# Attention scores and products with v take turns on all eight PSUM banks; weight loads are paced; one engine rounds q and k

## The chip, the core and the metric

The kernel runs on one core of a Trainium2 chip. Its time is the device time of the program in microseconds, the median of several runs; one execution is also taken by the hardware profiler. A core has TensorE (PE; its weight loads are listed as PEld), VectorE (DVE), ScalarE (ACT), GpSimd (POOL, idle here) and SyncE (SP, whose queue issues every DMA here). TensorE writes to PSUM, which has eight banks of 2 KB for each of 128 partitions; one matmul output of 512 fp32 columns fills a bank.

## What is computed

Sigmoid attention over 8 batches, 12 heads, 448 positions and 64 columns, followed by a gated MLP over the 3584 rows:

```python
scores = np.matmul(q, k.transpose(0, 1, 3, 2)) / np.sqrt(64) - np.log(448)
attn = 1.0 / (1.0 + np.exp(-scores))
x = np.matmul(attn, v).transpose(0, 2, 1, 3).reshape(3584, 768)
h = x @ w_in                                # 768 x 2048
g = h * (1.0 / (1.0 + np.exp(-1.702 * h)))
out = g @ w_out                             # 2048 x 768
```

The weights reach the kernel as 64-bit words; it decodes them to fp32 on the chip.

## The kernel before, in words

**The planner.** Nothing is issued while the code walks the loops. Each step becomes a task with an engine (or two to choose from, `either`), an estimated cost, the tasks that it needs and the buffers that it uses. Buffers of one tag form a ring: with BUFS[tag] slots, a buffer's users wait for all users of the one that many places earlier (lines 104 to 106). `Plan.run` (line 92) then plays the tasks through a model of the engines and emits each engine's instructions in the order in which the model begins them, which is the fixed order of that engine's queue on the chip. TensorE takes units in order from two streams, the attention ("side") and the MLP ("main"). Another engine takes, among the tasks that are ready, the one with the smallest key: its place in TensorE's order, or that of the first task that waits for it (`keys`, line 228). VectorE prefers tasks that only it can do (line 190), unless a task with a smaller key than that, and due within SOON places of TensorE's current one, is ready or nearly so (lines 193 to 199). The model lets a DMA land 2.2 us after its transfer, counted at 0.0027 us for each KB, and 1.5 us later still for the 64-bit weights (lines 46 and 387).

**The attention** handles 48 pairs of heads (8 batches by 6 pairs). A pair's q and k arrive as one tile (`qkraw`, line 479) and are split into a rounded part (line 340 on ScalarE or 341 on VectorE, by the planner's choice) and the rest (line 346, VectorE), so that three matmuls of fp32r make one precise product; only the very first pair is multiplied unsplit. The scores of a pair are made in four chunks of 112 keys: each is 6 matmuls, two heads side by side on 64 rows each, into a double bank (line 518). One sigmoid for each chunk (line 529) goes from the double bank to SBUF tile `a` (3 buffers of two chunks). The product with v (line 541, 16 matmuls on all four chunks, two heads side by side on 64 columns each) follows one pair later: a unit of TensorE's order is the four chunks of scores of pair n, then the product of pair n - 1. One or two copies (line 575 on ScalarE or 577 on VectorE) take it from PSUM to the blocks of x, which are 512 rows and so don't coincide with batches; finished blocks are spilled to DRAM.

PSUM holds two double banks `sc` and one `sc3`, which the chunks take in turn (every third one `sc3`), and the single banks `av` and `m0`, which the products with v take in turn. That makes all eight. After the attention `sc3` is closed and gives two single banks `m`; the MLP's first block takes `m0`, `m`, `m` in turn.

**The weights** come in 32 pieces, 16 for the down matrix first, then 16 (index below NF) for the up matrix. `decode` (line 372) loads a piece of 768 KB into one of three `raw64` buffers, makes it fp32 in seven VectorE steps (one of them free to go to ScalarE) and one of ScalarE (line 397), and stores it to DRAM (`stored`, line 430). The load waits for its buffer alone; its key is that of a pair's rounding, pair 2 + int(1.3 x piece). In the attention, sums and differences of down pieces are also made, split and stored (line 642), for a Strassen-like scheme in the later blocks.

**The MLP** is one block of 512 rows by plain products (`mlp`, lines 686), then three rounds of two blocks by seven products in place of eight (`two_blocks`, lines 918 and 1059).

Of the kernel before, what the change touches and what calls it, by code (L numbers as in the profile page):

```python
# [9 lines left out]
F32 = mybir.dt.float32  # L10
# [6 lines left out]
U64 = mybir.dt.uint64  # L17
# [7 lines left out]

PACE = 1.3

# [6 lines left out]
BUFS = dict(  # L34
    qk=2, vraw=3, a=3, x32=8, x=6, g=16, line=4, wsplit=3, raw64=3, w32=2, e=3,
    sc=2, sc3=1, av=1, m=2, m0=1,
    xs=15, xa=4,
)

ATTENTION, LATE = ("qk", "vraw", "a", "raw64", "e"), ("xs", "xa")  # L40
SHARED = ("line",)


# [199 lines left out]
def sigmoid_attention_mlp(ctx: ExitStack, tc: tile.TileContext, qk, v, w, out):  # L243
# [30 lines left out]

    for tag in ("sc", "av", "m0"):
        banks(tag, ctx)
    banks("sc3", early_bank)
    ctx.callback(early_bank.close)
# [20 lines left out]
    nc.vector.memset(still, 1.0)  # L299
    ps = spaces["m0"].tile([P, 512], F32, tag="m0", name="still", bufs=BUFS["m0"])  # L300
    for n in range(WARM):
# [4 lines left out]
    def make(b, tag, shape, dtype, name):  # L306
        if tag == "m" and tag not in spaces:
            early_bank.close()
            banks(tag, early_bank)
        if tag in LATE and tag not in spaces:  # L310
            att_stack.close()
            late = late_stack.enter_context(tc.tile_pool(name="late", bufs=2))
            for t in LATE:
                spaces[t] = late
        b.tile = spaces.get(tag, sb).tile(shape, dtype, tag=tag, name=name, bufs=BUFS[tag])
        return b.tile
# [20 lines left out]
    def round_and_rest(costs, b, src, deps, uses, hi, lo, first=lambda: None):  # L337

        c = on_either(
            (costs[0], lambda: nc.scalar.copy(hi(), src())),  # L340
            (costs[1], lambda: nc.vector.tensor_copy(hi(), src())),
            deps, [b, *uses], first,
        )
        return task(
            "DVE", costs[2],
            lambda: nc.vector.tensor_tensor(lo(), src(), hi().bitcast(F32), op=ALU.subtract),  # L346
            [c], [b, *uses],
        )
# [23 lines left out]
    def decode(n):  # L372
# [12 lines left out]

        load = dma(lambda: raw.tile.bitcast(U64), lambda: w[n], 2 * KB, [], [raw], take)
        load.landing += 1.5
        plan.early.append((load, firsts[min(2 + int(PACE * len(decoded)), len(firsts) - 1)]))

# [39 lines left out]
        decoded[n] = (t_p, f, f32)  # L429
        stored[n] = dma(lambda: whole[n], f32, KB, [t_p], [f])  # L430

# [53 lines left out]
    def split_pair(b, p, t_q, qkr):  # L485
        if (b, p) == (0, 0):
            return t_q, qkr
        s = buffer("qk")
        t = round_and_rest(
            (0.94, 0.63, 1.09), s, lambda: qkr.tile, [t_q], [qkr],  # L490
            lambda: s.tile[:, 0], lambda: s.tile[:, 1],
            lambda: make(s, "qk", [P, 2, S2], F32R, f"qk{b}_{p}"),
        )
        return t, s


    chunks = itertools.count()
    last_early = []

    def scores(b, p, c, t_s, s, a):  # L500

        tag = "sc"
        if next(chunks) % 3 == 2:
            tag = "sc3"
        ps = buffer(tag)
        if tag == "sc3":
            last_early[:] = [ps]

# [4 lines left out]
        def emit():  # L513
            make(ps, tag, [P, 2, 512], F32, f"sc{b}_{p}_{c}")
            src = [s.tile] if plain else [s.tile[:, 0], s.tile[:, 1]]
            for n, (kk, qq) in enumerate(terms):
                for j, rows in enumerate(halves_of_rows):
                    nc.tensor.matmul(  # L518
                        ps.tile[:C, j, :S],
                        lhsT=src[kk][rows, S + c * C : S + (c + 1) * C], rhs=src[qq][rows, :S],  # L520
                        start=n == 0, stop=n == len(terms) - 1,
                    )

        t = task("PE", 0.9 if plain else (0.7, 0.61, 0.61, 0.7)[c], emit, [t_s], [ps, s])

# [8 lines left out]

    def values(b, p, c, t_a, a, t_v, vr, ps, bank):

        def emit():
            if c == 0:
                make(ps, bank, [P, 512], F32, f"av{b}_{p}")
            for j, cols in enumerate(halves_of_rows):  # L540
                nc.tensor.matmul(  # L541
                    ps.tile[cols, :S], lhsT=vr.tile[:C, j, c], rhs=a.tile[:C, c % 2, j],
                    start=c == 0, stop=c == NC - 1,
                )

        return task("PE", (0.8, 0.75, 0.75, 0.85)[c], emit, [t_a, t_v], [ps, a, vr])
# [24 lines left out]
    def to_x(b, p, t, ps):  # L571
        for block, xb, first, into, cols in x32_places(b, p):
            n = cols.stop - cols.start
            wrote[block, p].append(on_either(
                (0.2 + 0.00075 * n, lambda xb=xb, into=into, cols=cols: nc.scalar.copy(
                    xb.tile[:, into], ps.tile[:, cols])),
                (0.15 + 0.00105 * n, lambda xb=xb, into=into, cols=cols: nc.vector.tensor_copy(
                    xb.tile[:, into], ps.tile[:, cols])),
                [t], [xb, ps], first,
            ))  # L580
        split_x(b, p)
# [20 lines left out]
    def attention():  # L602

        units, late = [], []
        for n, (b, p) in enumerate(pairs):
            t_q, qkr, t_v, vr = load_pair(b, p)
            t_s, s = split_pair(b, p, t_q, qkr)
            bank = "av" if n % 2 else "m0"
            ps = buffer(bank)
            scored, next_late = [], []  # L610
            firsts.append(t_s)
            for half in range(2):
# [3 lines left out]
                next_late.append([  # L616
                    values(b, p, 2 * half + i, g[1], a, t_v, vr, ps, bank) for i, g in enumerate(got)
                ])

            for t in scored[1]:  # L620
                t.alone = False
            units.append(scored[0] + scored[1] + [t for two in late for t in two])
            to_x(b, p, next_late[1][1], ps)
            late = next_late
        units.append(late[0] + late[1])
        return units
# [47 lines left out]
    def product_bank():  # L674

        n = next(groups)
        return ("m", last_early[0].users if n < 3 else []) if n % 3 else ("m0", [])

    def mlp(b):
# [11 lines left out]
        for f in range(NF):  # L691
            t_w, wb = wsplit(f)
            bank, edge = product_bank()
            ps = buffer(bank)
            g, gb = buffer("line"), buffer("g")
            for part in range(3):
                ks = range(2 * part, 2 * part + 2)

                def emit(ks=ks, part=part, ps=ps, bank=bank, wb=wb, f=f):
                    if part == 0:  # L700
                        make(ps, bank, [P, 512], F32, f"h{b}_{f}")
                    for k in ks:
                        product(ps.tile, wb.tile, k, xs[b, k][1].tile, k == 0, k == NK - 1)

# [5 lines left out]

            def sigmoid(g=g, ps=ps, f=f):
                make(g, "line", [P, T], F32, f"g{b}_{f}")
                nc.scalar.activation(g.tile, ps.tile, AF.Sigmoid, scale=1.702)

            t = task("ACT", 0.6, sigmoid, [t], [g, ps])
            t = task(
                "DVE", 0.69,
                lambda g=g, ps=ps: nc.vector.tensor_tensor(g.tile, ps.tile, g.tile, op=ALU.mult),
                [t], [g, ps],
# [452 lines left out]
```

## Time and profile before

| | us |
|---|---|
| median of 3 runs | 1117.43 (1116.3 to 1117.65) |
| the profiled execution | 1117.21 |
| its span, first to last instruction | 1115.4 |
| TensorE busy | 1107.6 |
| VectorE busy | 759.4 |
| ScalarE busy | 508.1 |
| attention, until the MLP's first matmul | 295.5 |

A row of busy time gives its share of the span. The attention, the first block of the MLP and the three rounds of two blocks follow one another on TensorE. Matmuls are pipelined: a matmul's record is longer than the time until the next one starts, so a busy TensorE is not proof that it steps at full pace, and starts have to be compared.

### The profile page before, as it was taken

The page shows a single profiled execution, that of the slowest core. Times are in us where ns is not written, and L with a number is a line of the kernel's source. Part 1 is how long each engine was busy: PE and PEld are TensorE (multiplying, and loading weights), DVE is VectorE, ACT ScalarE, POOL GpSimd, SP SyncE. Part 2 cuts the span into 40 slices and gives each one's busy share as a digit, 9 for nine tenths or more (in the row PEclk, how much of TensorE's full clock was granted, in tenths as well). Part 3 has the DMA queues.
Part 4 walks back from the last instruction along what each step waited for, and adds up shares of the span by engine and source line. Part 5 has one row for each costly group of instructions (what it writes and reads, how often), then busy time and mean ns, then how long its engine had stood idle before and what let it go on. Part 6 is the DMA issues. An engine that isn't in the chain of part 4 may idle for free.

```text
span 1115.4 us, 14973 instructions
## 1 busy us (share of the span) xinstructions
PE 1107.6 (99%) x5517; PEld 819.6 (73%) x5517; DVE 759.4 (68%) x1234; ACT 508.1 (46%) x729; POOL 0.2 (0%) x4
## 2 busy tenths in 40 slices
PE   8999999999999999999999999999999999999998
PEld 3544544545688888888888888888888888888887
DVE  6999999895496426887984664448864744477652
ACT  6988988888563322223633222225432322244220
POOL 0000000000000000000000000000000000000000
PEclk9999999999999999999999999999999999999999
DMA  9999999995455968666777975567669755556665
GB/s 330 333 375 375 388 400 395 385 338 162 151 188 182 358 216 321 246 244 216 254 227 223 307 242 191 195 198 250 216 208 310 255 188 191 195 174 214 207 202 194
DMA packets 113097, 285.69 MB, mean 256 GB/s; under 512 B 10368, under 2 KB 51328, under 8 KB 113024
## 3 DMA queue, kind: packets, MB, share of 16 engines
q1 hardware_dynamic: 113024, 284.73, 74.6%
q8 instruction: 44, 0.72, 0.3%
q14 instruction: 29, 0.24, 0.1%
HBM read 206.05 MB, written 78.64 MB: 255 GB/s over the span
## 4 chain that ended last, share of the span: by engine, by line
PE 96%; ACT 1%; DMA 1%; issue 0%; DVE 0%; SPq 0%; ACTq 0%; DVEq 0%
PE os L1059 18%; PE m L918 18%; PE oa L1059 13%; PE av L541 13%; PE sc L518 11%; PE sc L918 9%; PE h L686 6%; PE o L686 6%; PE av L918 4%; DMA qkraw<-qk 1%; ACT a L529 1%; SPq L321 0%; ACT sign L397 0%; DVE qk L346 0%; ACT qk L340 0%
## 5 line engine op out<-in xcount | busy, mean ns | idle before, releaser
L529 ACT ACTIVATE a<-sc,bias 112x896 f32<-112x896 f32 x192 | 183.0, 1006 | 42.8 <-PE av L541 30.4
L1059 PE MATMUL os<-gs,wds 128*128 128x512 f32 x864 | 196.3, 389 | 0.0
L1059 PEld LDWEIGHTS os<-gs,wds 128*128 128x128 f32 x864 | 162.2, 188 | 33.7
L541 PE MATMUL av<-a,vraw 112*64 112x448 f32 x768 | 154.7, 545 | 0.0
L1059 PE MATMUL oa<-ga,wda 128*128 128x512 f32 x648 | 147.4, 389 | 0.0
L1059 PEld LDWEIGHTS oa<-ga,wda 128*128 128x128 f32 x648 | 121.6, 188 | 25.3
L518 PE MATMUL sc<-qk 64*112 64x448 f32 x1128 | 137.4, 378 | 2.2 <-ACT a L529 2.1
L518 PEld LDWEIGHTS sc<-qk 64*112 64x112 f32 x1128 | 90.9, 171 | 63.3 <-ACT a L529 52.0
L541 PEld LDWEIGHTS av<-a,vraw 112*64 112x64 f32 x768 | 50.9, 136 | 82.3 <-issue 73.4
L918 PE MATMUL m<-x_s,w 128*128 128x512 f32 x468 | 109.3, 389 | 0.0
L918 PE MATMUL sc<-x,w 128*128 128x512 f32 x432 | 105.7, 389 | 0.0
L918 PEld LDWEIGHTS m<-x_s,w 128*128 128x128 f32 x468 | 87.8, 188 | 18.2
L918 PEld LDWEIGHTS sc<-x,w 128*128 128x128 f32 x432 | 81.1, 188 | 16.8
L880 ACT ACTIVATE g<-h 128x512 f32<-128x512 f32 x72 | 44.7, 632 | 91.1 <-DVE h L781 90.3
L340 ACT CAST gs<-gs 128x512 fp32r<-128x512 f32 x75 | 46.6, 623 | 84.5 <-PE os L1059 74.5
L686 PE MATMUL h<-x,wsplit 128*128 128x512 f32 x288 | 65.6, 389 | 0.0
L686 PE MATMUL o<-gs,wsplit 128*128 128x512 f32 x288 | 65.4, 389 | 0.0
L686 PEld LDWEIGHTS h<-x,wsplit 128*128 128x128 f32 x288 | 54.0, 188 | 11.9 <-issue 0.7
L686 PEld LDWEIGHTS o<-gs,wsplit 128*128 128x128 f32 x288 | 54.1, 188 | 11.2
L346 DVE TENSOR_TENSOR gs<-gs,gs 128x512 fp32r<-128x512 f32 x96 | 60.9, 686 | 0.4
L885 DVE TENSOR_TENSOR gs<-sc,g 128x512 f32<-128x512 f32 x24 | 16.6, 692 | 60.6 <-ACT g L880 60.6
L346 DVE TENSOR_TENSOR qk<-qkraw,qk 128x896 fp32r<-128x896 f32 x47 | 51.2, 1089 | 6.2 <-ACT qk L340 5.5
(94 smaller groups left out, 1204.1 us busy)
## 6 DMA issues: line engine op xcount, KB each, us to landing
w<-w SPq DMA_DIRECT2D x56, 768.0 KB, 6.6
wds<-t SPq DMA_DIRECT2D x72, 384.0 KB, 4.1
t<-t SPq DMA_DIRECT2D x32, 768.0 KB, 5.4
w<-t SPq DMA_DIRECT2D x32, 768.0 KB, 5.0
qkraw<-qk SPq DMA_DIRECT2D x48, 448.0 KB, 9.3
wda<-w SPq DMA_DIRECT2D x48, 384.0 KB, 4.0
f<-w SPq DMA_DIRECT2D x32, 384.0 KB, 8.1
w<-wsplit SPq DMA_DIRECT2D x16, 768.0 KB, 6.1
```

Source lines behind the costliest of these rows:

```text
L340: (costs[0], lambda: nc.scalar.copy(hi(), src())),
L346: lambda: nc.vector.tensor_tensor(lo(), src(), hi().bitcast(F32), op=ALU.subtract),
L518: nc.tensor.matmul(ps.tile[:C, j, :S], lhsT=src[kk][rows, S + c * C : S + (c + 1) * C], rhs=src[qq][rows, :S], start=n == 0, stop=n == len ...
L529: nc.scalar.activation(a.tile[:C, c % 2], ps.tile[:C, :, :S], AF.Sigmoid, bias=bias[:C], scale=scale)
L541: nc.tensor.matmul(ps.tile[cols, :S], lhsT=vr.tile[:C, j, c], rhs=a.tile[:C, c % 2, j], start=c == 0, stop=c == NC - 1,)
L686: nc.tensor.matmul(ps, lhsT=ws[a], rhs=x[:, c], start=first and i == 0, stop=last and i == 2)
L880: nc.scalar.activation(g.tile, h(), AF.Sigmoid, scale=1.702)
L885: nc.vector.tensor_tensor(gb.tile[:, block - one], h(), g.tile, op=ALU.mult)
L918: nc.tensor.matmul(ps, lhsT=ws[c], rhs=x[:, d], start=not more and i == 0 and j == 0, stop=i == NK // 2 - 1 and j == 2, skip_group_check=more,
L1059: nc.tensor.matmul(to, lhsT=w[c], rhs=x.tile[:, d], start=not more and i == 0 and j == 0, stop=i == len(rows) - 1 and j == 2, skip_group_c ...
```

## The change

- The chunks of scores and the products with v share one rotation over four double banks, in the order in which the units are formed: `sc`, `sc`, `sc3`, `sc4`. A product takes the turn after the four chunks of the next pair. `av`, `m0` and `m` are opened when the first MLP product needs one; by then `sc3` and `sc4` are closed. The MLP's first product takes a bank of `sc`, and the three after it wait for the last users of `sc3` and `sc4`.
- q and k are rounded by VectorE alone (cost None for ScalarE).
- A weight load is due with pair 2 + int(1.45 x piece) and waits for the rounding of pair int(1.45 x piece) - 1.
- The store of a piece of the up matrix waits for the rounding of the sixth last pair.
- The exponent buffers `e` are four in place of three; some of the planner's costs change; the planner looks only at a unit's first two chunks of scores to decide when it can begin.

```diff
-PACE = 1.3
+PACE, LEAD = 1.45, 1
+LATEST = 6
...
-    qk=2, vraw=3, a=3, x32=8, x=6, g=16, line=4, wsplit=3, raw64=3, w32=2, e=3,
-    sc=2, sc3=1, av=1, m=2, m0=1,
+    qk=2, vraw=3, a=3, x32=8, x=6, g=16, line=4, wsplit=3, raw64=3, w32=2, e=4,
+    sc=2, sc3=1, sc4=1, av=1, m=2, m0=1,
...
+EARLY, SINGLE = ("sc3", "sc4"), ("m0", "av", "m")
...
-    for tag in ("sc", "av", "m0"):
-        banks(tag, ctx)
-    banks("sc3", early_bank)
+    banks("sc", ctx)
+    for tag in EARLY:
+        banks(tag, early_bank)
...
-        if tag == "m" and tag not in spaces:
+        if tag in SINGLE and tag not in spaces:
             early_bank.close()
-            banks(tag, early_bank)
+            for t in SINGLE:
+                banks(t, early_bank)
...
-        load = dma(lambda: raw.tile.bitcast(U64), lambda: w[n], 2 * KB, [], [raw], take)
+        pair = int(PACE * len(decoded))
+        load = dma(lambda: raw.tile.bitcast(U64), lambda: w[n], 2 * KB, [firsts[pair - LEAD]] if pair >= LEAD else [],
+                   [raw], take)
         load.landing += 1.5
-        plan.early.append((load, firsts[min(2 + int(PACE * len(decoded)), len(firsts) - 1)]))
+        plan.early.append((load, firsts[min(2 + pair, len(firsts) - 1)]))
...
-        stored[n] = dma(lambda: whole[n], f32, KB, [t_p], [f])
+        stored[n] = dma(lambda: whole[n], f32, KB, [t_p, *(firsts[-LATEST:][:1] if n < NF else [])], [f])
...
-            (0.94, 0.63, 1.09), s, lambda: qkr.tile, [t_q], [qkr],
+            (None, 0.63, 1.09), s, lambda: qkr.tile, [t_q], [qkr],
...
+    def two_banks(b):
+        b.tag = ("sc", "sc", *EARLY)[next(turns) % 4]
+        plan.rings.setdefault(b.tag, []).append(b)
+        last_early[b.tag] = b
...
     def scores(b, p, c, t_s, s, a):
-        tag = "sc"
-        if next(chunks) % 3 == 2:
-            tag = "sc3"
-        ps = buffer(tag)
+        ps = Buffer()
+        two_banks(ps)
...
-            for t in scored[1]:
+            if n:
+                two_banks(before)
+            before = ps
+
+            for t in scored[1] + [t for two in late for t in two]:
                 t.alone = False
...
+        two_banks(before)
         units.append(late[0] + late[1])
...
-        return ("m", last_early[0].users if n < 3 else []) if n % 3 else ("m0", [])
+        if not n:
+            return "sc", []
+        edge = [t for tag in EARLY for t in last_early[tag].users] if n < 4 else []
+        return ("m0", "m", "m")[(n - 1) % 3], edge
```

## Rows read from the trace of the kernel before

**Rows 1.** The page's busy times and its chain of work that ended last.
```profile
PE 1107.6 (99%) x5517; PEld 819.6 (73%) x5517; DVE 759.4 (68%) x1234; ACT 508.1 (46%) x729; POOL 0.2 (0%) x4
...
PE 96%; ACT 1%; DMA 1%; issue 0%; DVE 0%; SPq 0%; ACTq 0%; DVEq 0%
```

**Rows 2.** Stretches: length, busy us (instructions) by engine, granted clock, DMA share, GB/s.
```profile
0.00:295.50 295.50, 291.34 (x1918) 144.04 (x1918) 243.70 (x409) 246.76 (x302) 0.20 (x4) 1.00 0.91 333
103.20:151.10 47.90, 47.90 (x324) 24.02 (x322) 44.84 (x77) 43.51 (x57) 0.00 (x0) 1.00 1.03 395
247.40:295.50 48.10, 48.10 (x315) 23.24 (x313) 23.34 (x37) 34.99 (x40) 0.00 (x0) 1.00 0.44 141
295.50:1111.80 816.30, 816.27 (x3602) 675.57 (x3600) 514.97 (x824) 261.38 (x427) 0.00 (x0) 1.00 0.69 229
```

**Rows 3.** Scores' matmuls (ns min/median/max) and the sigmoid's group (busy us, mean ns).
```profile
L518 PE MATMUL sc<-qk x1128: 355/363/460, 7.7 to 289.0; 64*112 64x448 f32 x188
...
L529 ACT ACTIVATE a<-sc,bias 112x896 f32<-112x896 f32 x192 | 183.0, 1006 | 42.8 <-PE av L541 30.4
```

**Rows 4.** Timeline of TensorE in the attention: start, us, merged matmuls [idle before].
```profile
7.75 3.56 PE L518 MATMUL sc<-qk 64*112 64x448 f32 x24
11.23 3.23 PE L541 MATMUL av<-a,vraw 112*64 112x448 f32 x16
...
20.36 0.86 PE L518 MATMUL sc<-qk 64*112 64x448 f32 x6
...
25.14 3.23 PE L541 MATMUL av<-a,vraw 112*64 112x448 f32 x16
...
46.27 2.09 PE L518 MATMUL sc<-qk 64*112 64x448 f32 x18
48.61 0.87 PE L518 MATMUL sc<-qk 64*112 64x448 f32 x6 [0.25 <-ACT a L529]
...
100.41 2.88 PE L518 MATMUL sc<-qk 64*112 64x448 f32 x24
103.22 3.23 PE L541 MATMUL av<-a,vraw 112*64 112x448 f32 x16
106.38 2.90 PE L518 MATMUL sc<-qk 64*112 64x448 f32 x24
```

**Rows 5.** Timeline of TensorE's weight loads in the run at 100.41.
```profile
100.41 1.69 PEld L518 LDWEIGHTS sc<-qk 64*112 64x112 f32 x18 [0.70 <-ACT a L529]
102.44 0.47 PEld L518 LDWEIGHTS sc<-qk 64*112 64x112 f32 x6 [0.34 <-ACT a L529]
```

**Rows 6.** Timeline of ScalarE around the same run.
```profile
100.88 0.27 ACT L575 COPY x<-av 128x128 f32<-128x128 f32 x1
101.38 1.91 ACT L529 ACTIVATE a<-sc,bias 112x896 f32<-112x896 f32 x2 [0.23 <-PE sc L518]
103.17 0.42 ACT L575 COPY x<-av 128x320 f32<-128x320 f32 x1
...
105.06 1.91 ACT L529 ACTIVATE a<-sc,bias 112x896 f32<-112x896 f32 x2 [0.62 <-PE av L541]
```

**Rows 7.** Waits of weight loads, 28.3 to 295.5: us in total, times, longest.
```profile
PEld sc L518 <- ACT a L529: 46.7, 88, 0.7
```

**Rows 8.** Waits of the whole span, same columns.
```profile
DVE x L577 <- ACT x L575: 1.5, 4, 0.5
```

**Rows 9.** Groups that round q and k; the chain and ScalarE's timeline at the start.
```profile
L340 ACT CAST qk<-qkraw 128x896 fp32r<-128x896 f32 x20 | 18.9, 944 | 0.4
L341 DVE CAST qk<-qkraw 128x896 fp32r<-128x896 f32 x27 | 16.9, 626 | 18.8 <-PE sc L518 9.6 <-DMA qkraw<-qk 9.0
...
4.12 11.94 DMA qkraw<-qk
...
20.24 0.93 ACT L340 CAST qk<-qkraw 128x896 fp32r<-128x896 f32 x1
```

**Rows 10.** DMA issues from 26 to 247 us: count, KB each, median us to landing.
```profile
w<-w SPq DMA_DIRECT2D x28, 768.0 KB, 9.0
```

## What the change should do to the time

> **What bounds the kernel now.** I read the page first: TensorE is busy 99% of the span, and the chain that ended last is 96% TensorE [rows 1]. So only time in which TensorE stands, or steps slower than it could, is to be had. The stretches split it [rows 2]: from 295.5 to 1111.8 us TensorE is busy 816.27 of 816.30, and the change leaves the order of that part as it is; the attention before it holds 291.34 of 295.50. By busy time nothing is left there either, but a matmul's record is longer than its step (0.363 us each [rows 3], yet 24 of them in 2.8 us), so a short wait between two disappears under the record of the one before. I therefore went by starts in TensorE's timeline [rows 4].
>
> A scores run of one pair is 12 steps of two matmuls side by side (two heads). The first three chunks, where they stand alone (18 matmuls, 2.09 us), have their last start 2.09 - 0.36 = 1.73 us after the first; the opening three steps alone (6 matmuls, 0.86 us) have it at 0.50. So a step costs (1.73 - 0.50) / 6 = 0.205 and an opening step 0.30. Chunk four could begin at 1.73 + 0.20 = 1.93 and the run end after three more steps, 0.20 + 0.20 + 0.29 (the turn to the values), at 2.62. The regular run takes 103.22 - 100.41 = 2.81. The weight loads show where the rest goes [rows 5]: those of chunk four begin at 102.44, 2.03 us into the run, after 0.34 us of idle time ended by the sigmoid of line 529. That sigmoid is chunk one's: it starts at 101.38 and takes 1.006 us [rows 3, 6], so it ends at 102.39. With three double banks for scores, chunk four takes the bank that chunk one has just filled. The wait costs 0.10, and since the first weights of chunk four are then loaded with nothing ahead of them, another opening step costs 0.09: 0.19 to 0.20 us for each pair. It is regular: between 28.3 and 295.5 us weight loads waited 88 times for that line, 46.7 us in all [rows 7], twice for each of 44 runs, 44 x (0.70 + 0.34) = 45.8; the rest, 0.9 us, is three longer waits. The 0.70 stands at the head of a run, under the last values. The row names a sigmoid there too, but the bank's own, of the pair before's chunk two, ended at 101.38 + 1.91 = 103.3, 3 us before the run at 106.38 [rows 4, 6], so I count no gain there.
>
> **The change, part by part.**
>
> *Banks.* Scores and products with v now take four double banks in turn: five uses for each pair (four chunks, then the pair before's product). Chunk four gets the bank that the product of two pairs back has left; the product gets that of the same pair's chunk one; chunks one to three get those of the pair before's chunks two to four. Each against its need, in us from the run's start: the product begins at 2.62 and chunk one's sigmoid ends at 102.39 - 100.41 = 1.98 [rows 6], a margin of 0.6; chunk three begins at 1.32 and the sigmoids of the pair before's chunks three and four (105.06, 1.91 us for both) end at 106.97, 0.59 after the next run's start at 106.38 [rows 4, 6], a margin of 0.7; chunk two and one have more. Chunk four at 1.93 needs both copies of the product that ended as the run began. The wait of 0.19 to 0.20 goes away in 45 runs (the 44 and the one at 14.39): 9.0 us. The three longer waits are of the kind at 48.61: 48.61 - 46.27 = 2.34 against 2.03, 0.31 more each [rows 4]: 0.9 us.
>
> *The copies* are the new wait on the path: ScalarE's queue has sigmoids behind it, VectorE's has the decoding of weights, and TensorE's chunk four waits for them. Today nobody needs that bank for a pair, and the second copy of the pair at 100.41 runs at 103.17, after two sigmoids, to end 3.18 us into the run [rows 6]; the first ends at 0.74. In the planner a task inherits the place of whoever waits for it, so both copies now stand ahead of decoding; the first on ScalarE (0.74) or the second directly behind it (0.42 more, 1.2) meets 1.93. I take them one after the other, since VectorE's copies waited four times for ScalarE's [rows 8]. Bounds: 0, and 3.18 - 1.93 = 1.25 in each of about 42 pairs with two copies. I take one pair in eight late by 0.3: 1.8 us. It is nearest to the first, since ScalarE's idle time and a free engine are there, and the planner knows the need.
>
> *The turns* between scores (64 rows by 112) and values (112 by 64) stay: none is removed or added. Had the idle 0.70 at the head of a run been a wait for a bank, as its row says, its cost would be like chunk four's, 0.19 in 46 runs, 8.7 us more, and the time 1098; the 3 us above speak against it. The Trainium skill ("TensorEngine Tiling (Array Packing)", section "Key Properties") has another cause for a loss at that place: changing the tiling mode drains TensorE. By that rule the turn costs the same with any banks and the sum has none of the 8.7; by the name in the row it would have all of it. The run heads after the change will tell.
>
> *q and k.* Twenty roundings leave ScalarE (0.944 us each, 18.9 us) and cost VectorE 0.626 each, 12.5 us [rows 9]. VectorE's 243.7 us of the attention [rows 2] become 256.2 of about 284: 90%, on average free, though it stood at 44.84 of 47.90 in the fuller stretches. The cover is the last 48 us, where it has 24.8 us idle; should weights slip, they slip into that. The rounding itself has a pair of time in hand (two buffers). ScalarE falls to 228 of 284. One of the twenty is on the path: at 20.24, directly before the sigmoids that the run at 20.36 waits for [rows 9].
>
> *The start.* The run at 20.36 takes until 25.14, 4.78 us against 2.62 [rows 4], 2.16 lost: a q/k load issued at 4.12 landed 11.94 us later, so VectorE was late, and ScalarE's rounding stood ahead of the sigmoids [rows 9]. Weights now wait for the rounding of the pair before, and ScalarE rounds nothing, so I count all of it (bounds 0 and 2.16). The run at 7.75 takes 3.48, 0.86 too many, for the three banks filled by the first pair's sigmoids; with four, half of it stays, because the first product then waits for the second pair's first sigmoid: gain 0.4.
>
> *Weights.* The last of 32 is due with pair 46 in place of 42 (2 + 1.45 x 31), and is asked for at pair 43's rounding, which can begin when pair 41's scores end, six pairs of 5.78 before the last scores' end at 278: some 245 us; with 9.0 us to land [rows 10] and its share of VectorE, 243.7 / 32 = 7.6 us, it is decoded by 262, before the 284 at which the MLP begins and long before its own turn there. Sixteen stores of 384 KB (6.3 MB) move into the last 48 us: 141 + 131 = 272 GB/s against 395 carried elsewhere [rows 2]. I cost both at nothing. If the stores come in one burst, 6.3 MB are 16 us at 395 GB/s, ahead of v loads with some 14 us in hand (three buffers: two pairs and a scores run): 2 us for one or two pairs, to the range.
>
> *Sum.* 9.0 + 0.9 + 2.2 + 0.4 = 12.5, less 1.8: 10.7 us. The profiled execution took 1117.21 (1115.4 span and 1.8 around it), the median of the runs is 1117.43: 1106.5, with the 284.8 at which the attention would end.
>
> **The rivals.** *Copies late as a rule:* the second copy stays behind sigmoids or decoding in half of the pairs, by 0.2 to 0.3, which gives back 4 to 6 us: 1109 to 1112.5. For it: the order of today [rows 6]. Against: the bank's new users raise its place. *No bank wait after all:* the step of 0.19 belongs to the chunk's place and stays; only the start gains, 1114 to 1115. Against: the idle time ends 0.05 after a sigmoid does, and chunks two and three begin without it. *VectorE held up by a weight (slower):* loads go out one pair ahead, the planner counts 5.8 us to land (2.2 + 1.5 + 768 x 0.0027), the rows 9.0 [rows 10]; VectorE's queue then stands at the weight with the copies behind it, which have 1.93 - 1.2 = 0.7 in hand. In the later 16 weights, with VectorE less full, 2.2 us late would cost 16 x 1.5 = 24 and leave 1117.2 - 12.5 + 24 = 1129. It decides from 0.7 + 12.5 / 16 = 1.5 us of lateness. Against: three weight buffers stay, and full queues on VectorE cover most of it. *Run heads gain too:* 1098, as worked out at the turns. *The clock:* today it is 1.00 in each stretch [rows 2], its upper level of 2.4 GHz, through every wait of the attention. At the lower level, 1.2 GHz, the attention's 280 us would double, to about 1390; nothing in the rows points there. The Trainium skill ("TensorE: Matmul & The Clock Gate", section "A second HAM failure mode: psum-queue depth-cycling") tells of cycling through banks with short idle times that made the clock swing. By it this change could do so; no run here shows it, since three banks with a wait for each pair kept 1.00.
>
> **How the numbers follow.** Forecast (1103.5 to 1108.5) 0.62; run heads too 0.02; late copies or the v loads (to 1113) 0.17; no bank effect 0.04; VectorE held up with nothing left of the gain, 0.06 within 0.2% and 0.08 slower; clock 0.01. The lower end takes every loss as gone (13.0) and 0.7 for the spread of runs (1116.3 to 1117.65); the upper takes the late copies in: 1103.5 to 1113. A measurement of this kernel tells 0.2% (2.2 us) from none: faster 0.85, same 0.06, slower 0.09.
>
> **What would show it.** Scores runs of 2.62 from start to start of the values; no idle time of weight loads at chunk four ended by line 529; a pair every 5.78 in place of 5.97; the MLP's first matmul near 284.8 in place of 295.5; no rounding of q and k on ScalarE; the run at 20 us without its 2.2. I would be wrong if chunk four's wait comes back with a copy of line 575 or 577 as its end, if VectorE stands at weights with TensorE idle behind, or if the MLP's matmuls start late.

## The result, and the profile after

The changed kernel takes 1107.86 us (median of 4 runs, 1107.53 to 1108.83), the kernel before 1117.33 beside it: a ratio of 0.9918, 95% interval 0.9901 to 0.9935. Forecast were 1106.5 and the range 1103.5 to 1113. The profiled execution has a span of 1107.0 us against 1115.4, 8.4 less.

TensorE's timeline of the changed kernel shows the regular pair (start, length, merged matmuls; line 534 makes scores, 557 the products with v):

```profile
150.04 2.70 PE L534 MATMUL sc<-qk 64*112 64x448 f32 x24
152.68 3.23 PE L557 MATMUL av<-a,vraw 112*64 112x448 f32 x16
155.84 2.70 PE L534 MATMUL sc<-qk 64*112 64x448 f32 x24
158.47 3.23 PE L557 MATMUL av<-a,vraw 112*64 112x448 f32 x16
```

From the start of scores to that of the values it is 152.68 - 150.04 = 2.64, and 2.63 in the next pair, where [rows 4] had 2.81; a pair takes 5.80. The weight loads of the same run, line by line as in [rows 5]:

```profile
155.83 2.31 PEld L534 LDWEIGHTS sc<-qk 64*112 64x112 f32 x24 [0.70 <-ACT a L545]
```

All 24 loads stand in one row: the idle time of 0.34 ahead of chunk four is gone. The starts show what it cost. In the median of the 35 runs of pairs 8 to 42, chunk four's first two steps started 0.311 and 0.298 us after the step before them; now it is 0.204 and 0.206, like the other steps, so 0.20 us less in each run. The 0.70 at the head of the run is as before, although the banks now change hands in another order. Of the 46 runs from the third pair on, 41 take 2.61 to 2.64. The five others are these two and three of the same kind, at 78.36 (2.95), 102.43 (2.79) and 178.98 (2.75):

```profile
84.47 2.08 PE L534 MATMUL sc<-qk 64*112 64x448 f32 x18
86.80 0.87 PE L534 MATMUL sc<-qk 64*112 64x448 f32 x6 [0.24 <-ACT x L591]
...
114.18 2.08 PE L534 MATMUL sc<-qk 64*112 64x448 f32 x18
117.18 0.86 PE L534 MATMUL sc<-qk 64*112 64x448 f32 x6 [0.92 <-DVE x L593]
```

In both, chunk four waits for a copy of the product of two pairs back (line 591 on ScalarE, 593 on VectorE), the wait that the change added. The five runs lose 2.4 us together. Why the copy at 117 was late stands in VectorE's timeline (in brackets the idle time ahead of an instruction, and what ended it):

```profile
111.82 0.56 DVE L676 TENSOR_TENSOR w<-w,w 128x384 f32<-128x384 f32 x1 [0.86 <-DMA f<-w]
112.29 0.62 DVE L347 CAST qk<-qkraw 128x896 fp32r<-128x896 f32 x1
113.93 0.56 DVE L676 TENSOR_TENSOR w<-w 128x384 f32<-128x384 f32 x1 [1.02 <-DMA f<-w]
114.41 1.08 DVE L358 TENSOR_TENSOR qk<-qkraw,qk 128x896 fp32r<-128x896 f32 x1
...
116.35 0.68 DVE L593 COPY x<-av 128x128 f32<-128x128 f32 x2
```

VectorE stood twice, 1.9 us in all, until a decoded weight had been read out to DRAM; only then could it write differences of weights in its place. The copies stood behind that in its queue and began 2.17 us into the run that needed them by 1.93. Ahead of the run at 78 it had stood for a weight that had not landed yet:

```profile
76.32 0.56 DVE L435 TENSOR_SCALAR w<-w 128x768 uint32<-128x768 uint32 x1 [1.72 <-DMA w<-w]
```

Ahead of the run at 179 it was ScalarE that stood for a load, 0.75 us. Ahead of the other two, at 84 and 102, neither queue stood for a transfer; VectorE was full.

Stretches of the changed kernel (length, busy us by engine as in [rows 2], clock, DMA share, GB/s):

```profile
0.00:286.20 286.20, 282.84 (x1917) 148.25 (x1917) 248.71 (x418) 247.19 (x293) 0.20 (x4) 1.00 0.96 344
247.40:295.50 48.10, 48.10 (x305) 27.53 (x302) 30.18 (x51) 33.74 (x42) 0.00 (x0) 1.00 0.77 279
```

The MLP's first matmul comes at 286.2 and not at 295.5: 9.3 us earlier. The last 48 us of the old attention now carry 279 GB/s, not 141, and the new attention's own last 48 us 298. Two places went the other way, and neither was forecast:

```profile
4.43 4.80 PE L534 MATMUL sc<-qkraw 64*112 64x448 f32 x16 [0.64 <-DMA qkraw<-qk]
8.72 2.95 PE L534 MATMUL sc<-qk 64*112 64x448 f32 x24
...
435.91 2.33 PE L945 MATMUL sc<-x,w 128*128 128x512 f32 x9 [0.42 <-DVE h L966]
```

The first pair's scores take 8.72 - 4.43 = 4.29 us where they took 7.75 - 4.25 = 3.50, and begin 0.18 later; in the MLP TensorE waits for a copy out of PSUM, which with smaller hitches costs 0.85 against the kernel before. Neither is a fixed cost of the change: in the same kernel's repetition, below, the MLP takes no longer than in the kernel before, and the first pair's pace differs between executions of one program.

### The profile page after: what moved, and what is told of

It reads as the page before. It is cut to its first block, busy times and chain, and to the rows that moved or that the text cites. A ratio compares the mean times of both kernels' runs of the same rounds, so it can differ in the third digit from the quotient of the medians.

```text
span 1107.0 us, 14927 instructions
## 1 busy us (share of the span) xinstructions
PE 1099.6 (99%) x5517; PEld 823.7 (74%) x5517; DVE 762.2 (69%) x1241; ACT 510.4 (46%) x722; POOL 0.2 (0%) x4
## 4 chain that ended last, share of the span: by engine, by line
PE 92%; DMA 4%; DVE 3%; SPq 1%; issue 0%; ACT 0%; DVEq 0%
PE os L1086 18%; PE m L945 17%; PE oa L1086 13%; PE av L557 11%; PE sc L534 10%; PE sc L945 8%; PE h L709 6%; PE o L709 5%; PE av L945 4%; DMA w<-w 2%; DMA wf<-f 1%; DMA f<-w 1%; SPq L326 1%; DMA qkraw<-qk 0%; DVE w L442 0%; DVE qk L358 0%
## 5 line engine op out<-in xcount | busy, mean ns | idle before, releaser
L534 PEld LDWEIGHTS sc<-qk 64*112 64x112 f32 x1128 | 94.9, 171 | 48.5 <-ACT a L545 30.5
L534 PE MATMUL sc<-qk 64*112 64x448 f32 x1128 | 128.1, 371 | 1.2 <-DVE x L593 0.9
L808 DVE TENSOR_TENSOR h<-h,m 128x512 f32<-128x512 f32 x36 | 24.7, 685 | 39.7 <-PE m L945 39.6
```

The source lines that it names most:

```text
L534: nc.tensor.matmul(ps.tile[:C, j, :S], lhsT=src[kk][rows, S + c * C : S + (c + 1) * C], rhs=src[qq][rows, :S], start=n == 0, stop=n == len ...
L808: nc.vector.tensor_tensor(out(), a(), b(), op=op)
```

## The experiments

They ran in three groups of four, in the order of the table, each beside the kernel before, whose medians were 1116.87, 1117.14 and 1117.37. Where the MLP begins is read from each profile, which is of one execution and not of the median; the length from there to the end is 819.9 us in the kernel before and 820.8 in the profile of the changed one.

| kernel | us (median, range) | ratio, 95% | MLP begins | from there |
|---|---|---|---|---|
| rotation alone | 1113.38 (1111.67 to 1115.27) | 0.9968, 0.9956 to 0.9980 | 285.8 | 827.7 |
| all but the rotation | 1116.04 (1115.12 to 1116.91) | 0.9992, 0.9983 to 1.0000 | 295.1 | 820.0 |
| changed, loads don't wait | 1107.04 (1106.83 to 1107.32) | 0.9910, 0.9896 to 0.9923 | 285.5 | 820.0 |
| changed, 8 warming matmuls | 1107.60 (1107.16 to 1109.47) | 0.9917, 0.9904 to 0.9931 | 286.1 | 819.9 |
| changed, either engine rounds | 1112.65 (1109.98 to 1113.58) | 0.9952, 0.9939 to 0.9966 | 284.8 | 826.6 |
| changed, 3 exponent buffers | 1107.97 (1105.83 to 1109.59) | 0.9918, 0.9904 to 0.9931 | 285.8 | 819.9 |
| rotation, VectorE rounds, 4 exponent buffers | 1112.47 (1110.07 to 1114.27) | 0.9955, 0.9942 to 0.9967 | 290.4 | 820.1 |
| loads don't wait, 8 warming matmuls | 1107.37 (1105.84 to 1109.72) | 0.9915, 0.9902 to 0.9929 | 284.0 | 820.0 |
| changed, stores at once | 1110.28 (1108.67 to 1111.27) | 0.9939, 0.9926 to 0.9951 | 287.8 | 820.0 |
| changed, pace 1.3, loads don't wait | 1106.82 (1105.94 to 1108.00) | 0.9910, 0.9896 to 0.9923 | 285.7 | 819.9 |
| changed, again | 1108.84 (1107.98 to 1110.11) | 0.9928, 0.9915 to 0.9940 | 286.4 | 819.9 |
| changed, loads don't wait, again | 1106.30 (1105.95 to 1107.19) | 0.9907, 0.9892 to 0.9922 | 284.0 | 820.1 |

### The rotation alone, and everything else alone

```diff
 rotation alone, against the changed kernel:
-PACE, LEAD = 1.45, 1
+PACE, LEAD = 1.3, 1
-... e=4,
+... e=3,
-[firsts[pair - LEAD]] if pair >= LEAD else []
+[]
-[t_p, *(firsts[-LATEST:][:1] if n < NF else [])]
+[t_p]
-(None, 0.63, 1.09), s, lambda: qkr.tile
+(0.94, 0.63, 1.09), s, lambda: qkr.tile
```

> Only the rotation of scores and products over four double banks; weights asked for as before (pace 1.3, no wait for a rounding, stores at once, three exponent buffers), q and k rounded by either engine. Theory (the bank wait of chunk four is what was gained): scores runs from start to start of the values 2.62 us in nearly all pairs as in the changed kernel, the MLP's first matmul between 286 and 290 us, 1108 to 1111 us; the stall near 20 us may stay (up to 2.2). Rival (even weight loads and the rounding on one engine gained it): runs stay at 2.81 and the time near 1116 to 1117.

> Everything but the rotation: banks as before (three double banks for scores, two single ones for products), pace 1.45 with the wait for a rounding, late stores, four exponent buffers, q and k rounded by VectorE alone. Theory: runs of 2.81 us, weight loads idle 0.34 at chunk four in each, the stall near 20 us gone; 1114.5 to 1116.5 us. Rival (these parts gained it): 1108 to 1110.

With everything but the rotation the old wait is there, here in the weight loads of two runs (line 540 is the sigmoid of this kernel):

```profile
150.28 0.48 PEld L529 LDWEIGHTS sc<-qk 64*112 64x112 f32 x6 [0.34 <-ACT a L540]
154.23 1.69 PEld L529 LDWEIGHTS sc<-qk 64*112 64x112 f32 x18 [0.70 <-ACT a L540]
156.26 0.48 PEld L529 LDWEIGHTS sc<-qk 64*112 64x112 f32 x6 [0.33 <-ACT a L540]
```

It gains 0.8 us, which its interval (to 1.0000) hardly tells from none. Its run at 22 us takes 2.82, so the stall of the start is gone here too, but its first pair stepped slowly for longer than in most other profiles. So the rotation is what shortens the runs, and the rival that the other parts did it falls. With the rotation go the planner's changed costs for scores and its look at a unit's first two chunks; they were not tried apart from it.

The rotation alone did not do as expected (1108 to 1111). Its attention ends at 285.8, all of the gain, and then the MLP's first block gives 7.8 us back in this execution, the slowest of the six. TensorE's timeline there (line 709 is h; 745 is VectorE's gating):

```profile
285.76 28.86 PE L709 MATMUL h<-x,wsplit 128*128 128x512 f32 x126
316.49 6.00 PE L709 MATMUL h<-x,wsplit 128*128 128x512 f32 x18 [1.88 <-DVE g L745]
324.63 25.67 PE L709 MATMUL h<-x,wsplit 128*128 128x512 f32 x105 [2.14 <-DVE g L745]
```

Two stretches of the same kernel, with columns as in [rows 2]:

```profile
285.80:300.00 14.20, 14.20 (x65) 11.76 (x64) 13.69 (x24) 8.01 (x12) 0.00 (x0) 1.00 0.97 373
...
317.70:321.20 3.50, 3.50 (x10) 2.69 (x10) 3.50 (x6) 1.73 (x2) 0.00 (x0) 0.52 0.93 370
```

VectorE is full (13.69 of 14.20) and the product of h with its sigmoid comes 1.9 and 2.1 us late. After each of the two waits the granted clock fell to about half for some microseconds (0.52 in the stretch at 317.7). The last of the 32 weights was decoded at 328 us in this kernel, 257 in the kernel before, 273 in the changed one: what VectorE owed in the attention it did in the MLP.

### Which part keeps the weights up

```diff
 either engine rounds, against the changed kernel:
-(None, 0.63, 1.09), s, lambda: qkr.tile
+(0.94, 0.63, 1.09), s, lambda: qkr.tile
 three exponent buffers, against the changed kernel:
-raw64=3, w32=2, e=4,
+raw64=3, w32=2, e=3,
```

> The changed kernel, but q and k rounded by either engine as before. The rotation alone ended its attention at 285.8 us, 9.7 earlier, and then lost 7.8 in the MLP's first block, because weights were decoded at one in some 11.5 us and not 8. Theory: ScalarE has one free stretch of some 1.6 us in a pair, which holds either a sign (0.93, needed once for each weight, ScalarE only) or a rounding (0.94); with roundings there signs come in every other pair. So weights fall behind again here: last decode after the MLP has begun, TensorE idle in the first block, 1110 to 1115 us. Rival (three exponent buffers, or the loads' pace, held the weights up there): decode ends near 270 as in the changed kernel, 1107 to 1109.

> The changed kernel with three exponent buffers as before in place of four. A weight holds two of them from its first step to the product of exponent and sign, so three keep the next weight's sign from starting early. Theory (ScalarE's free stretch is what held weights up): decode ends by 285 and the time is within 1 us of the changed kernel, 1107 to 1109. Rival (the buffers held weights up): decode runs into the MLP, 1110 to 1115.

Three exponent buffers change nothing (1107.97, last decode at 269). Rounding by either engine does: last decode at 333, two waits in the MLP's first block again:

```profile
315.57 4.39 PE L709 MATMUL h<-x,wsplit 128*128 128x512 f32 x18 [1.86 <-DVE g L745]
322.15 8.23 PE L709 MATMUL h<-x,wsplit 128*128 128x512 f32 x28 [2.19 <-DVE g L745]
```

That kernel's ScalarE, in order of time (line 412 is the sign of a weight, 352 a rounding, 545 the sigmoid):

```profile
104.59 0.93 ACT L412 ACTIVATE sign<-w 128x768 bf16<-128x768 int16 x1
106.23 1.91 ACT L545 ACTIVATE a<-sc,bias 112x896 f32<-112x896 f32 x2 [0.71 <-PE av L557]
108.58 1.91 ACT L545 ACTIVATE a<-sc,bias 112x896 f32<-112x896 f32 x2 [0.44 <-PE sc L534]
110.38 0.94 ACT L352 CAST qk<-qkraw 128x896 fp32r<-128x896 f32 x1
112.08 1.91 ACT L545 ACTIVATE a<-sc,bias 112x896 f32<-112x896 f32 x2 [0.77 <-PE av L557]
114.37 1.91 ACT L545 ACTIVATE a<-sc,bias 112x896 f32<-112x896 f32 x2 [0.38 <-PE sc L534]
116.17 0.94 ACT L352 CAST qk<-qkraw 128x896 fp32r<-128x896 f32 x1
```

Between chunk two's sigmoid and chunk three's, which waits for the values to give an `a` buffer back, there are 106.23 - 104.59 = 1.64 us, and one operation of 0.93 in each, with 0.7 unused. In the kernel before a stretch of 38.95 - 37.06 = 1.89 us held both:

```profile
37.06 0.93 ACT L397 ACTIVATE sign<-w 128x768 bf16<-128x768 int16 x1
37.88 0.94 ACT L340 CAST qk<-qkraw 128x896 fp32r<-128x896 f32 x1
38.95 1.91 ACT L529 ACTIVATE a<-sc,bias 112x896 f32<-112x896 f32 x2
```

In the median over pairs 6 to 44, from the end of chunk two's sigmoid to the start of chunk three's, the stretch is 1.77 us in the kernel before and 1.58 in this one, shorter by the 0.19 that a run lost to the wait for chunk four. In those 39 pairs this kernel's stretch holds a rounding 20 times, a sign 19 times, and never both.

That roundings on ScalarE make the weights late once the rotation is in is shown by the run. That the stretch, now too short for a sign and a rounding, is the reason is read from these rows; no run lengthened it alone.

### Pace, late stores, and the wait of a load

```diff
 rotation, VectorE rounds, four exponent buffers, against the changed kernel:
-PACE, LEAD = 1.45, 1
+PACE, LEAD = 1.3, 1
-[firsts[pair - LEAD]] if pair >= LEAD else []
+[]
-[t_p, *(firsts[-LATEST:][:1] if n < NF else [])]
+[t_p]
 stores at once:                           the last of these three
 loads don't wait:                         the second
 pace 1.3, loads don't wait:               the first and the second
```

> The rotation, q and k on VectorE alone, four exponent buffers; pace 1.3 as before, no wait of a load for a rounding, stores at once. Theory: rotation and rounding are all of the gain, pace and late stores are worth under 1 us: 1106.5 to 1108.5, decode done near 255 us. Rival (even asking keeps data transfers from delaying q, k and v): a stall or late copies worth 2 us and more, 1109 to 1112.

> The changed kernel, with the stores of up pieces issued as soon as a piece is decoded. Rotation, rounding on VectorE and four exponent buffers alone lost 4 to 5 us against the changed kernel, in scores runs from 207 to 250 us where the DMA engines were full and the second copy of a product stood behind a sigmoid. Theory: the late stores are what kept that stretch clear, so long runs between 150 and 250 us come back: 1109 to 1112. Rival (the pace of 1.45 with its wait did it): within 1 us of the changed kernel.

> The changed kernel with pace 1.3 and no wait of a load for a rounding; late stores stay. Theory (late stores matter, the pace does not): 1107 to 1108.5, no long runs after 150 us. Rival (the pace matters): long runs between 150 and 250 us, 1109 to 1112.

> The changed kernel without the wait of a weight load for the rounding of a pair (pace 1.45 stays). Theory: the five long runs of the changed kernel (78, 84, 102, 114, 179 us; 2.4 us in all) come from VectorE standing at a weight that was asked for late, with the copies of the product behind it; without the wait they go, the idle time of VectorE that ends with a weight's landing falls, and the time is 1105 to 1106.5, unless the q/k load at the start comes late again (then 1107 to 1108.5). Rival (copies are late because VectorE is full, not because it stands): the long runs stay, 1107.5 to 1108.5.

Without all three, 1112.47: the MLP begins at 290.4, since scores runs from 207 us on are long. One is 4.48 us:

```profile
207.63 2.09 PE L534 MATMUL sc<-qk 64*112 64x448 f32 x18
211.30 0.87 PE L534 MATMUL sc<-qk 64*112 64x448 f32 x6 [1.58 <-ACT x L591]
```

In the timeline of its ScalarE, one copy that the next run needs:

```profile
217.14 0.25 ACT L591 COPY x<-av 128x128 f32<-128x128 f32 x1
```

The scores of that pair began at 215.26: the copy stands behind chunk one's sigmoid and ends 2.13 into the run, with 1.93 needed. That is the rival of copies late as a rule; the six runs that follow, up to 250 us, are 0.2 to 0.8 us too long.

Putting back the early stores alone loses about a third as much, 1110.28 against 1108.84 for the changed kernel repeated. In that kernel's stretch from 200 to 247 us DMA moved 387 GB/s and TensorE stood for 1.5 us:

```profile
200.00:247.00 47.00, 45.51 (x314) 23.87 (x312) 43.27 (x75) 37.94 (x45) 0.00 (x0) 1.00 1.03 387
```

The changed kernel's has 364 GB/s and no standing:

```profile
200.00:247.00 47.00, 47.00 (x328) 24.96 (x326) 45.03 (x75) 41.92 (x53) 0.00 (x0) 1.00 1.03 364
```

With stores at once, one run takes 4.28 us, and its wait is again for a copy, this time VectorE's, as TensorE's timeline of that kernel shows:

```profile
222.17 0.86 PE L534 MATMUL sc<-qk 64*112 64x448 f32 x6 [1.42 <-DVE x L593]
```

With late stores, pace 1.3 and no wait of loads it is 1106.82, and the same stretch again has no standing:

```profile
200.00:247.00 47.00, 47.00 (x326) 24.98 (x324) 44.93 (x75) 42.26 (x54) 0.00 (x0) 1.00 1.00 361
```

This kernel and the one at 1112.47 differ by the stores alone. So late stores are worth 1.4 us beside the pace and the wait of loads, and 5.7 without them. The pace and the wait together are worth 2.2 us while stores go at once (1112.47 against 1110.28) and nothing once they are late. How the early stores make the copies late, by the transfers that they hold up or by the order of work that the planner then chooses, is not shown. Intervals of single kernels are about 1.4 us to either side, so the order of these is firmer than the sizes.

The wait of a load for a rounding probably costs something. Without it the five long runs became four, 1.8 us together, where I had expected them to go; the time was 0.8 lower, in another group and with intervals that overlap, and the second time 2.5 lower.

> The changed kernel itself, on the same chip as the run without the wait of loads: 1107.0 to 1108.5, five long scores runs between 78 and 179 us again if they come from the order of the queues, others if they come from when transfers land.

> The changed kernel without the wait of loads for a rounding, beside the changed kernel: if the wait costs something, 0.5 to 1.5 us faster than it (1106.5 to 1107.5); if not, the same within 0.3 us.

Repeated, the changed kernel took 1108.84, 0.3 more than the range expected, and had four long runs (85, 91, 115 and 179 us), not the same five: which copies are late is not settled by the order of the queues alone. Beside it, the kernel without the wait of loads was 2.5 us faster, 1.0 more than expected. Of the 2.1 us between the two profiled executions, though, 2.0 lie ahead of the first product, which began at 10.55 and not at 12.59, because the first pair stepped slowly for a shorter time:

```profile
7.59 2.95 PE L534 MATMUL sc<-qk 64*112 64x448 f32 x24
10.55 0.97 PE L557 MATMUL av<-a,vraw 112*64 112x448 f32 x4
```

From the first product to the MLP the two differ by 0.3 us (273.8 with the wait, 273.5 without), and the changed kernel and the first run without the wait by 0.5 (274.6 and 274.1). One long run of 3.87 us lost nearly as much, 1.2 us, as the four with the wait, 1.5. VectorE's waits for weights from 25 to 280 us (us, times, longest) are in the changed kernel:

```profile
DVE w L435 <- DMA w<-w: 4.5, 5, 1.7
```

and in the repetition without the wait of loads:

```profile
DVE w L435 <- DMA w<-w: 1.2, 2, 0.8
```

In the first run without the wait of loads this row read 4.9 us, and that kernel was faster too. So asking earlier is no loss, twice; a gain is likely, since each execution with the wait was slower than each of those without it that it is compared with, but the profiles place only 0.3 to 0.5 us of it behind the first pair, and that it acts by VectorE's wait is not shown.

### The first pair

```diff
-WARM = 5
+WARM = 8
```

> The changed kernel with eight warming matmuls at the start in place of five. Theory: the first pair's scores in the changed kernel step at 0.75 us for four steps, against 0.376 from the third step on in the kernel before, because TensorE stood longer ahead of them; with three more matmuls (0.43 us each) that end near 5.1 us they start 0.5 to 0.7 us later but step at 0.376 throughout: 1107.2 to 1107.7. Rival (the late rise of the clock has to do with the matmuls since 4.4 us alone): as the changed kernel or up to 0.7 slower, 1107.9 to 1108.6.

> A version meant to be faster than the changed kernel: loads don't wait for a rounding (measured alone at 1107.0) and eight warming matmuls (1107.6; its first product began 0.74 us earlier, while it lost more to late copies). If both add up: first product near 10.9 us, MLP near 284.7, 1106.2 to 1106.8. If the plan shifts and late copies come back elsewhere: 1107 to 1108.

```profile
1.48 3.60 PE L306 MATMUL still<-still 128*128 128x512 bf16 x8 [1.48 <-DVE still L303]
5.00 3.41 PE L534 MATMUL sc<-qkraw 64*112 64x448 f32 x16
7.90 2.95 PE L534 MATMUL sc<-qk 64*112 64x448 f32 x24
10.86 1.35 PE L557 MATMUL av<-a,vraw 112*64 112x448 f32 x6
```

With eight the scores begin 0.6 later and the first product 0.74 earlier than in the changed kernel (10.86 against 11.60): they step at full pace from the second step on. But late copies took 2.9 us in that kernel's profile, and its time is 1107.60. Both edits together have the earliest MLP of all, 284.0, in the profile (1105.84), and 1107.37 in the median. The sum of both gains was not reached.

The version that came out lowest each time is the changed one without the wait of loads: 1107.04 and 1106.30, and with pace 1.3 1106.82, against 1107.86 and 1108.84.

## Why the prediction was right, step by step

The whole, 10.7 us, came out as 9.5 of the medians and 8.4 of the profiled spans. Of the sum's terms, by starts in the two timelines:

| term | forecast | measured |
|---|---|---|
| chunk four's wait | 9.0 | 8.9 |
| three longer waits | 0.9 | 0.9 |
| run at 20 us | 2.2 | 2.2 |
| run of the second pair | 0.4 | 0.6 |
| late copies | -1.8 | -2.4 |
| first pair's pace and q/k landing | 0 | -1.0 |
| the MLP | 0 | -0.85 |

The regular wait is the difference of all 46 runs, 132.83 - 123.22 = 9.61, with the 2.4 lost to late copies added and the 2.2 and 0.9 of the next two rows taken off. The last two rows are of one execution each and did not come back as they stand in the repetition: its MLP lost nothing, and its first pair took 1.9 us longer than the kernel before's.

*The bank wait* was right in place, size and cause: the idle time ended by the sigmoid is gone in the loads, the run is 2.61 to 2.64, and without the rotation it is back.

*The copies* were right as the new wait and 0.6 too small. The manner was wrong: I spread them over one pair in eight with 0.3 each; it was five pairs with up to 1.2. What I had as the slower rival, VectorE waiting for a weight to land with the copies queued behind, stood ahead of one of them (78 us); a wait for a weight's store, which I had not thought of, ahead of another (114), ScalarE's wait for a load ahead of a third (179), and ahead of the two others VectorE was just full. So of that rival the mechanism is in the profile, once, at 0.3 us.

*The turns.* The 0.70 at the head of a run stayed, with the same releaser named: no wait for a bank. That agrees with the cause that the Trainium skill gives ("TensorEngine Tiling (Array Packing)", section "Key Properties": changing the tiling mode drains TensorE), and no run here took a turn away. Of what a turn costs the starts tell this, alike in both kernels: the last step of the values takes 0.476 us where the others take 0.376, and the opening step of the scores 0.30 where the next take 0.20.

*The weights and q and k* are the step that failed, though the time does not show it. I costed the rounding, the pace and the stores at nothing, with the idle end of the attention as cover. The whole bears that out, decode done at 273 (262 forecast), 298 GB/s in the last 48 us (272 forecast). But this cover is made by those parts: without the rounding on VectorE it is gone, decode ends at 333, and the time is 1112.65; and with none of pace, wait and late stores the copies come late from 207 us on, at 1112.47, of which the late stores alone take back 5.7. I gave the banks all of the regular gain and would have forecast some 1108 for them alone; that is 1113.4, and all the rest alone 1116.0. The gain of 9.5 is no sum of the parts' (3.5 and 0.8). What I missed is that the rotation shortens the stretch in which ScalarE does its other work by the very time that it saves, from 1.77 to 1.58 us in the median, and that the stores of the up pieces go out while the DMA engines are full (share 1.03 from 200 to 247 us) unless they wait. The forecast of the whole came out because both repairs were part of the change, and not because I had priced what they repair.

*The start.* The stall at 20 us went, as counted, but its cause is open. It also went with ScalarE rounding and the loads waiting, and with loads not waiting; so neither of the two that I named is needed by itself. With neither, in the rotation alone, only 0.4 us were lost, at 26 us (a run of 3.00); and with all but the rotation it went too. The kernel before has one profile, so that the late q/k load was an accident of that execution is not excluded. The right number here is not a proof of the reason.

*The clock* as a rival (all of the attention slower) was no issue, 1.00 from the first rise on. The swings that the Trainium skill ("TensorE: Matmul & The Clock Gate", section "A second HAM failure mode: psum-queue depth-cycling") tells of for cycling through banks did not come in this attention. A fall after waits came in the MLP of two of the experiments: see below.

## What to carry to other kernels

Where matmuls overlap in the records, compare starts within a regular run: some 0.2 us in each of 45 pairs was 9 us, under a TensorE that looked 99% busy. When the bound engine is sped up by a little in each round, look at what the other engines did in the time that goes: here a ScalarE stretch that could hold two operations held one, and the debt appeared in the next stage. A buffer that becomes shared makes its slowest reader urgent: here five copies that stood behind other work in their queues cost 2.4 us. And a gain of 1 to 2 us in one execution may be its first microseconds: compare from a common point behind them before giving it to an edit.

## What the runs showed of the chip

*The first rise of the clock is late, and not at the same time in each execution.* The first pair's steps are 0.75 us (0.88 for the opening one) and then 0.376, twice as fast, which are TensorE's two levels of 1.2 and 2.4 GHz. The full step was reached after one slow step in the kernel before, four in the changed one and seven in its repetition, whose first pair took 9.70 - 4.32 = 5.4 us:

```profile
4.32 5.90 PE L534 MATMUL sc<-qkraw 64*112 64x448 f32 x16 [0.53 <-DMA qkraw<-qk]
9.70 2.96 PE L534 MATMUL sc<-qk 64*112 64x448 f32 x24
```

In each of them TensorE had stood for 0.46 to 0.64 us behind the five warming matmuls; with eight, in two profiles, its records show no standing and the slow steps were none or one. The length of the standing does not order them: 0.26 us in one of the experiments was followed by five slow steps. Over all fourteen profiles the first product began between 10.55 and 13.16 us. The column of the granted clock says 1.00 there, as its record begins with the rise; the steps tell it.

*A wait of 2 us in the MLP costs more than itself.* After each of the two waits in the rotation alone the steps were 0.427 us in place of 0.227 for about eight matmuls, with 0.52 in the clock's column, the lower level; 4.0 us of waits made 7.8 us of time. Of the six executions of that kernel the two whose mean granted clock was 1.000 took 1111.67 and 1112.18, the four at 0.997 and 0.998 took 1112.38 to 1115.27. With either engine rounding, the MLP's first wait, 1.86 us, was not followed by a fall (18 matmuls in 4.39 us) and its second, 2.19, was (28 in 8.23). In the attention no wait was followed by one; the longest there was 1.58 us. What divides them is not shown.
